# POOL's casts of the tokens of batches 4 to 7, put behind VectorE's last probabilities

## The chip, the cores and the metric

The kernel runs on one core of a Trainium2 chip. The metric is the device time of one execution in microseconds, the median of several runs. The engines of the core have a queue each and work in the order of their queue: TensorE (PE, matmuls; PEld is its weight load), VectorE (DVE), ScalarE (ACT), GpSimd (POOL) and SyncE (SP, which here only issues DMAs). They wait for one another through semaphores. The DMA engines, 16 of them, serve what SP, ACT and POOL issue.

## What is computed

A cross attention between 512 tokens and 32 state rows, for 8 batches of 8 heads with 64 elements each, and behind it a two-layer network over all rows:

```python
scores = scale * x @ state.T          # per batch and head: 512 x 32
a = softmax(scores);   xread = a @ state
scores2 = scale * state @ x.T         # 32 x 512
a2 = softmax(scores2); sread = a2 @ x
rows = concat([xread, sread], axis=2) # 544 rows per batch, heads side by side: 512 wide
h = rows @ w_in                       # 512 -> 2048
out = maximum(0.01 * h, h) @ w_out    # 2048 -> 512
```

Inputs and output are fp32; the kernel multiplies in bf16 and sums in fp32.

## The kernel before

Tokens are laid out with 128 partitions. For each batch the kernel does five things.

1. *Tokens.* `load_x` (L102) brings a batch's fp32 tokens (1 MB) into one of two buffers `xl`; `cast_all` (L135, POOL) casts them to bf16 into one of four buffers `xb`; `a_xt_dma` (L234, issued by SP) transposes those by DMA into one of two buffers `xT`.
2. *Scores.* `a_scores` (L256) multiplies `xT` with the transposed state into PSUM, all heads at once, 32 rows per head.
3. *Two softmaxes of these scores.* Over the state rows: `a_shift` (L266 to L276, VectorE), `a_exp` (L283, ScalarE), `a_probs` (L288 to L298, VectorE), which gives `aT`. Over the tokens: `a_max2` (L316, VectorE), `a_exp2` (L322, ScalarE), `a_probs2` (L330, L332, and L340 once per half, VectorE), which gives `a2`. `a_a2t` (L347, SP) transposes `a2` by DMA for `a_sread` (L365), the second attention's product.
4. *M.* `xread` is never formed: `a_m` (L392) multiplies the state with `w_in` into M, in four column blocks, and `m_evict` (L404 for two separate banks, L406 for a pair) casts each block from PSUM to bf16, on VectorE or ScalarE. So the first layer is `aT` times M.
5. *The network.* `ff1` (L413) makes one of 16 blocks of the hidden layer, with the leaky ReLU on ScalarE (L418); `piece` (L441) adds four of its blocks into a tile of the output; `y_store` (L450, L457) copies a finished tile out of PSUM and stores it through SP.

The order of every engine's queue is that of the program text: nothing is rescheduled. Batches 0 and 1 are written out by hand. Batches 2 to 7 run in a loop over `b` with 16 steps `s`. Step `s` of pass `b` issues `ff1` of batch b, then whatever stands under that step, then one `piece` of batch b - 1 or b. TensorE's queue is thereby dense, and what prepares the next batch, `nxt` = b + 1, is scattered over the steps:

- s = 0: the load of batch b + 2, on SP's queue in passes 2 and 3 and on POOL's in passes 4 and 5; the transposition of `a2` of batch b
- s = 1: scores of batch b + 1, the last block of M of batch b, `a_shift` and `a_max2` of batch b + 1, and in passes 2 to 5 the cast of batch b + 2
- s = 4, 6, 8: `a_sread` of older batches; in pass 2 also the load of the states of batches 4 to 7 (s = 4), and at s = 8 their cast on POOL (`state_cast`, L210) and their transposition by DMA (`state_t`, L215)
- s = 5 to 7: `a_exp`, `a_exp2`, then `a_probs` and `a_probs2` of batch b + 1
- s = 10: three blocks of M of batch b + 1 and their evictions, two of them on VectorE, the first of these being L404
- s = 13: the transposition of the tokens of batch b + 2

An engine isn't held to the step under which its instruction stands, only to its own queue and to the semaphores. POOL has nothing in the loop but the casts of L135, the state cast of pass 2 and the loads of passes 4 and 5, so it comes to each of them as soon as their data or buffer is there.

Of the kernel before, what the change touches and what calls it, by code (L numbers as in the profile page):

```python
# [9 lines left out]
P = 128  # L10
B, H, S, D = 8, 8, 512, 64
# [8 lines left out]
BF16 = mybir.dt.bfloat16  # L20
# [7 lines left out]
def kernel(  # L28
# [9 lines left out]
    nc = tc.nc  # L38

    consts = ctx.enter_context(tc.tile_pool(name="consts", bufs=1))  # L40
# [59 lines left out]
    def load_x(b, eng):  # L100
        xl[b] = xpool.tile([P, H, NT * D], FP32, name="xl", tag="xl", bufs=2)
        eng.dma_start(xl[b][:], x[b].rearrange("h (p t) d -> p h (t d)", t=NT))  # L102
# [11 lines left out]
    def open_xb(b):  # L114
        if b == 2:
            t = xpool.tile([P, 2, NT, NK, D], BF16, name="xb", tag="xb")
            xs[b] = [t[:, u] for u in range(2)]
        else:
            t = xpool.tile([P, NT, H, D], BF16, name="xb", tag="xb")
            xs[b] = [t[:, :, NK * u:NK * (u + 1)] for u in range(2)]  # L120
        xt[b] = t
# [9 lines left out]
            xl[b][:, h0:h1].rearrange("p h (t d) -> p h t d", t=NT),  # L131
        )

    def cast_all(b):
        nc.gpsimd.tensor_copy(  # L135
            xt[b][:].rearrange("p t h d -> p h t d"),
            xl[b][:].rearrange("p h (t d) -> p h t d", t=NT),
        )
# [61 lines left out]
    def load_state(i):  # L200
        lo, hi = groups[i]
        for k in range(NK):
            for g in range(2):
                nc.sync.dma_start(
                    stf[i][NS * k:NS * (k + 1), :, D * g:D * (g + 1)],
                    state[lo:hi, 2 * k + g].rearrange("b n d -> n b d"),
                )
# [6 lines left out]
    def state_t(i):  # L214
        nc.sync.dma_start_transpose(st_t[i][:], stb[i][:].rearrange("p b q -> p (b q)"))  # L215
# [36 lines left out]
    def a_scores(a):  # L252
        sc = psum.tile([P, 2, S], FP32, name="sc", tag="sc", bufs=1)
        for k in range(NK):
            for g in range(2):
                nc.tensor.matmul(  # L256
                    sc[NS * k:NS * (k + 1), g, :],
                    lhsT=st_of(a, g, k),
                    rhs=a.xTh[k // 2][D * g:D * (g + 1), :, k % 2, :],
                    start=True, stop=True,  # L260
                )
        a.sc = sc
# [40 lines left out]
    def a_shift(a):  # L303
        flat = a.sc[:].rearrange("p g c -> p (g c)")
        a.sh = block_sub(flat, block_max(flat, NB), NB)
# [8 lines left out]
    def a_max2(a):  # L314
        a.m2 = att.tile([P, 2], FP32, name="mcol", tag="mcol")
        nc.vector.tensor_reduce(out=a.m2[:], in_=a.sc[:], axis=AX.X, op=ALU.max, negate=True)  # L316
# [12 lines left out]
    def a_probs2(a):  # L329
        nc.vector.tensor_scalar(out=a.r2[:], in0=a.r2[:], scalar1=1e-9, scalar2=None, op0=ALU.add)  # L330
        q2 = att.tile([P, 2], FP32, name="qc", tag="qc")
        nc.vector.reciprocal(q2[:], a.r2[:])  # L332
        if a.b in (0, 6):
            pairs[a.b] = att.tile([P, 2, 2, S], BF16, name="a2p", tag="a2p", bufs=1)
        if a.b in (0, 1, 6, 7):
            a.a2 = pairs[a.b - a.b % 2][:, a.b % 2]
        else:
            a.a2 = att.tile([P, 2, S], BF16, name="a2", tag="a2", bufs=1)[:]
        for g in range(2):
            nc.vector.tensor_scalar(  # L340
                out=a.a2[:, g, :], in0=a.e2[:, g, :],
                scalar1=q2[:, g:g + 1], scalar2=None, op0=ALU.mult,
            )

    def a_a2t(a):
        t = att.tile([P, 2, NT, P], BF16, name="a2T", tag="a2T", bufs=1)
        nc.sync.dma_start_transpose(  # L347
            t[:].rearrange("p g i q -> p (g i) q"), a.a2.rearrange("p g s -> p (g s)")
        )
        a.a2T = t[:]  # L350

    def a_a2t_pair(b):
        t = att.tile([P, 2, 2, NT, P], BF16, name="a2pT", tag="a2pT", bufs=1)
        nc.sync.dma_start_transpose(
            t[:].rearrange("p b g i q -> p (b g i) q"),
            pairs[b][:].rearrange("p b g s -> p (b g s)"),
        )
        for v in range(2):
            att_of[b + v].a2T = t[:, v]
# [20 lines left out]
    def a_m(a, c, tag):  # L380
        if c == 0:
            a.M = mpool.tile([P, 2, DFF], BF16, name="M", tag="M")
        if tag in ("ph", "py", "phpy"):
            pm = [psum.tile([P, DM], FP32, name="pm", tag=t) for t in (tag[:2], tag[-2:])]
            at = [t[:] for t in pm]
        else:
            pm = psum.tile([P, 2, DM], FP32, name="pm", tag=tag, bufs=1)
            at = [pm[:, g, :] for g in range(2)]
        for k in range(NK):
            for g in range(2):  # L390
                v, r = (k // 2, 2 * (k % 2) + (g ^ (k // 2))) if a.b == 0 else (g, k)
                nc.tensor.matmul(  # L392
                    at[v][NS * r:NS * (r + 1)],
                    lhsT=st_of(a, g, k),
                    rhs=w_in_bf[D * g:D * (g + 1), k, DM * c:DM * (c + 1)],
                    start=True, stop=True,
                )
        return pm

    def m_evict(a, c, pm, copy):  # L400
        cols = slice(DM * c, DM * (c + 1))
        if isinstance(pm, list):
            for g in range(2):
                copy(a.M[:, g, cols], pm[g][:])  # L404
        else:
            copy(a.M[:, :, cols], pm[:])  # L406
# [3 lines left out]
    def ff1(a, hT, j):  # L410
        ph = psum.tile([P, S], FP32, name="ph", tag="ph")
        for g in range(2):
            nc.tensor.matmul(  # L413
                ph[:], lhsT=a.M[:, g, P * j:P * (j + 1)],
                rhs=a.aT[:, g, :],
                start=(g == 0), stop=(g == 1),
            )
        nc.scalar.activation(out=hT[:, j, :], in_=ph[:], func=AF.Prelu, scale=1 / SCALE, alpha=0.01)  # L418
# [387 lines left out]
    for b in range(2, B):  # L806
        hT = hpool.tile([P, 16, S], BF16, name="hT", tag="hT")
        a = att_of[b]
        nxt = att_of[b + 1] if b + 1 < B else None
        order = [(b - 1, i, 3) for i in range(2)]  # L810
        order += [(b - 1, i, jq) for i in range(2, NT) for jq in range(4)]
        order += [(b, i, jq) for jq in range(3) for i in range(2)]
        for s in range(16):
            ff1(a, hT, s)
            if s == 0:
                if b + 2 < B:
                    load_x(b + 2, nc.sync if b < 4 else nc.gpsimd)
                    open_xb(b + 2)
                if b == 7:
                    a_a2t_pair(6)  # L820
                elif b != 6:
                    a_a2t(a)
            elif s == 1:
                if nxt is not None:
                    a_scores(nxt)
                m_evict(a, 3, a_m(a, 3, "big"), SCA)
                if nxt is not None:
                    a_shift(nxt)
                    a_max2(nxt)
                if b + 2 < B:  # L830
                    cast_all(b + 2)
            elif s == 4:
                if b == 2:
                    load_state(1)
                    a_sread(a0)
            elif s == 6:
                if b in (2, 7):
                    a_sread(a1 if b == 2 else att_of[6])
            elif s == 8:
                if b != 6:  # L840
                    a_sread(a)
                if b == 2:
                    state_cast(1, nc.gpsimd)
                    state_t(1)
            if nxt is not None:
                if s == 5:
                    a_exp(nxt)
                elif s in (6, 7):
                    a_exp2(nxt, s - 6)
                    if s == 7:  # L850
                        a_probs(nxt)
                        a_probs2(nxt)
                elif s == 10:
                    pm0 = a_m(nxt, 0, "big")
                    pm2 = a_m(nxt, 2, "phpy")
                    pm1 = a_m(nxt, 1, "sc")
                    m_evict(nxt, 2, pm2, VEC)
                    m_evict(nxt, 0, pm0, VEC)
                    m_evict(nxt, 1, pm1, SCA)
                if s == 13 and b + 2 < B:  # L860
                    a_open(att_of[b + 2], b + 2)
                    a_xt_dma(att_of[b + 2])
            pb, i, jq = order[s]
            piece(pb, hT if pb == b else h_prev, i, jq)
        h_prev = hT
# [4 lines left out]
    b = B - 1  # L870
# [43 lines left out]
```

## Time and profile before

| | |
|---|---|
| runs before, us | 214.63, 214.82, 219.38 |
| median, us | 214.82 |
| profiled execution, us | 216.14 |
| its span, us | 214.1 |
| granted TensorE clock | 1.0 |
| HBM read, written | 17.30 MB, 8.91 MB |
| DMA, mean over the span | 129 GB/s |

The span runs from the first to the last instruction in the profile of one execution; the 2 us beside it lie before and behind them. Busy time of an engine, from the first part of the page: TensorE 206.1 us, VectorE 99.7, ScalarE 139.2, POOL 25.6. In a row of the timeline stand the start in us from the span's start, the duration in us, the engine, the line, the operation, the tile written <- the tiles read, the shapes and the number of instructions merged in the row; in square brackets, the engine's idle time before it and what ended that. In a row of grouped instructions stand the least, the median and the greatest duration in ns, then the first and the last start. SPq is SyncE's queue of DMA issues: its duration is that of the issue, not of the transfer. A row "DMA to landing" counts from the start of the issue to the landing.

### The profile page before, as it was taken

How to read it: one execution, taken by the hardware profiler on the slowest of the kernel's cores; microseconds unless marked ns; L12 is line 12 of the kernel's file. 1: busy time of each engine (PE TensorE's matmuls, PEld its weight loads, DVE VectorE, ACT ScalarE, POOL GpSimd, SP SyncE). 2: the span in 40 equal slices, each digit the busy share in tenths (PEclk: the TensorE clock that was granted, in tenths of full speed). 3: DMA queues.
4: the chain of work that ended last, by engine and by line, in shares of the span. 5: the costliest groups of instructions: out<-in, count | busy, mean ns of one | idle time of the engine just before them, and what ended most of it. 6: DMA issues, size and time to landing. Idle time of an engine off the chain costs nothing.

```text
span 214.1 us, 3696 instructions
## 1 busy us (share of the span) xinstructions
PE 206.1 (96%) x1485; PEld 96.4 (45%) x1510; DVE 99.7 (47%) x149; ACT 139.2 (65%) x263; POOL 25.6 (12%) x39
## 2 busy tenths in 40 slices
PE   7889999999999999989999999999999999999994
PEld 2533434343454444434454444444444444466643
DVE  2656797696959146951775085706581000000001
ACT  3578685898787477846696478747774766454420
POOL 8814000030032004503000000000000000000000
PEclk9999999999999999999999999999999999999999
DMA  6999999984962896387215221322023110111123
GB/s 192 211 207 298 254 253 126 239 226 100 240 157 75 176 258 189 139 237 157 95 52 133 64 100 52 91 56 99 35 74 90 52 73 25 49 52 49 49 52 98
DMA packets 38400, 27.70 MB, mean 129 GB/s; under 512 B 24560, under 2 KB 33136, under 8 KB 38384
## 3 DMA queue, kind: packets, MB, share of 16 engines
q1 hardware_dynamic: 32624, 18.75, 36.0%
q0 software_dynamic: 5376, 8.39, 17.7%
q10 hardware_dynamic: 384, 0.33, 0.7%
q8 instruction: 12, 0.20, 0.4%
q14 instruction: 4, 0.03, 0.1%
HBM read 17.30 MB, written 8.91 MB: 122 GB/s over the span
## 4 chain that ended last, share of the span: by engine, by line
PE 88%; DVE 4%; DMA 2%; ACT 2%; issue 1%; SPq 1%; ACTq 0%; DVEq 0%
PE py L441 48%; PE ph L413 21%; PE ph L424 3%; PE pyw L441 3%; PE pm L392 3%; DMA xf<-in_x_dram 2%; PE ph L661 2%; PE pyh L466 2%; PE psr L365 2%; PE php L661 1%; PE sc L256 1%; DVE r L330 1%; SPq L65 1%; PE scn L530 1%; DVE qb L297 1%
## 5 line engine op out<-in xcount | busy, mean ns | idle before, releaser
L441 PE MATMUL py<-w_out_bf,hT 128*128 128x512 bf16 x446 | 116.5, 379 | 1.6 <-DVE M L404 0.5
L418 ACT ACTIVATE hT<-ph 128x512 bf16<-128x512 f32 x112 | 66.5, 602 | 42.4 <-PE ph L413 41.7
L441 PEld LDWEIGHTS <-hT 128*128 128x128 bf16 x496 | 46.7, 98 | 57.6 <-issue 6.1
L413 PE MATMUL ph<-aT,M 128*128 128x512 bf16 x221 | 64.9, 379 | 0.2
L413 PEld LDWEIGHTS <-M 128*128 128x128 bf16 x224 | 21.7, 98 | 27.0 <-issue 1.4
L450 ACT COPY ysb<-py 128x512 f32<-128x512 f32 x31 | 18.1, 585 | 10.7 <-PE py L441 10.7
L266 DVE TRANSPOSE_TENSOR_REDUCE mrow<-sc 128x32 f32<-128x1024 f32 x7 | 8.8, 1250 | 33.2 <-PE sc L256 33.2
L471 DVE COPY ysh<-pyh 128x384 f32<-128x384 f32 x1 | 0.6, 558 | 49.0 <-PE pyh L466 49.0
L135 POOL CAST xb<-xl 128x2048 bf16<-128x2048 f32 x5 | 9.7, 1941 | 61.9 <-DMA xl<-in_x_dram 61.9
L288 DVE TRANSPOSE_TENSOR_REDUCE r<-e 128x32 f32<-128x1024 bf16 x7 | 8.7, 1245 | 11.5 <-ACT e L283 11.5
L406 ACT CAST M<-pm 128x1024 bf16<-128x1024 f32 x13 | 13.2, 1013 | 1.2 <-PE pm L392 0.7
L322 ACT ACTIVATE e<-sc,mcol 128x512 bf16<-128x512 f32 x16 | 11.2, 706 | 0.0
L316 DVE TENSOR_REDUCE mcol<-sc 128x2 f32<-128x1024 f32 x8 | 9.7, 1214 | 0.0
L428 ACT ACTIVATE hs<-ph 128x256 bf16<-128x256 f32 x16 | 6.0, 384 | 4.6 <-PE ph L424 4.4
L297 DVE STREAM_TRANSPOSE qb<-qh 128x1024 bf16<-128x1024 bf16 x7 | 8.7, 1246 | 0.2
L274 DVE STREAM_TRANSPOSE mrowb<-mrow 128x1024 f32<-128x1024 f32 x7 | 8.7, 1245 | 0.2
L276 DVE TENSOR_TENSOR sh<-sc,mrowb 128x1024 f32<-128x1024 f32 x7 | 8.6, 1224 | 0.2
L406 DVE CAST M<-pm 128x1024 bf16<-128x1024 f32 x7 | 8.5, 1216 | 0.2 <-PE pm L392 0.2
L424 PE MATMUL ph<-sr_t,w_in_bf 128*128 128x256 bf16 x64 | 8.3, 273 | 0.0
L404 DVE CAST M<-pm 128x512 bf16<-128x512 f32 x10 | 6.4, 684 | 3.2 <-PE pm L392 3.2
L392 PE MATMUL pm<-w_in_bf,st_t 64*32 64x512 bf16 x192 | 7.6, 379 | 0.0
L441 PE MATMUL pyw<-w_out_bf,hT 128*128 128x512 bf16 x31 | 7.5, 379 | 0.1
(103 smaller groups left out, 159.1 us busy)
## 6 DMA issues: line engine op xcount, KB each, us to landing
out_dram<-ysb SPq DMA_DIRECT2D x31, 256.0 KB, 2.4
xl<-in_x_dram SPq DMA_DIRECT2D x3, 1024.0 KB, 6.8
w_in_bf<-in_moe_w_in_dram POOLq DMA_DIRECT2D x4, 512.0 KB, 9.6
xl<-in_x_dram POOLq DMA_DIRECT2D x2, 1024.0 KB, 6.8
xf<-in_x_dram SPq DMA_DIRECT2D x4, 256.0 KB, 4.1
w_out_bf<-in_moe_w_out_dram POOLq DMA_DIRECT2D x4, 256.0 KB, 13.4
x<-in_x_dram POOLq DMA_DIRECT2D x2, 512.0 KB, 14.4
w_out_bf<-in_moe_w_out_dram POOLq DMA_DIRECT2D x2, 512.0 KB, 15.4
```

The source lines that it names most:

```text
L135: nc.gpsimd.tensor_copy(xt[b][:].rearrange("p t h d -> p h t d"), xl[b][:].rearrange("p h (t d) -> p h t d", t=NT),)
L266: nc.vector.tensor_reduce(out=m1[:], in_=flat.rearrange("p (c j) -> p c j", j=NS), axis=AX.X, op=ALU.max, apply_transpose=True,)
L297: nc.vector.transpose(q1b[:], q1h[:, :, None].to_broadcast([P, n, NS]))
L316: nc.vector.tensor_reduce(out=a.m2[:], in_=a.sc[:], axis=AX.X, op=ALU.max, negate=True)
L322: nc.scalar.activation(out=a.e2[:, g], in_=a.sc[:, g, :], func=AF.Exp, bias=a.m2[:, g:g + 1], accum_out=a.r2[:, g:g + 1],)
L392: nc.tensor.matmul(at[v][NS * r:NS * (r + 1)], lhsT=st_of(a, g, k), rhs=w_in_bf[D * g:D * (g + 1), k, DM * c:DM * (c + 1)], start=True, st ...
L406: copy(a.M[:, :, cols], pm[:])
L413: nc.tensor.matmul(ph[:], lhsT=a.M[:, g, P * j:P * (j + 1)], rhs=a.aT[:, g, :], start=(g == 0), stop=(g == 1),)
L418: nc.scalar.activation(out=hT[:, j, :], in_=ph[:], func=AF.Prelu, scale=1 / SCALE, alpha=0.01)
L424: nc.tensor.matmul(ph[:, :n], lhsT=w_in_bf[:, k, P * j:P * (j + 1)], rhs=sr_t[:, k, :], start=(k == 0), stop=(k == NK - 1),)
L441: nc.tensor.matmul(y.py, lhsT=hT[:, j, P * i:P * (i + 1)], rhs=w_out_bf[:, j, :], start=(j == 0), stop=(j == 15),)
L450: copy(ysb[:], ys[b, i].py)
```

## The change

`cast_all` gets a second argument. Where it is given, POOL first copies it into a one-column tile `turn` that nobody reads, and then casts. The call in the loop moves from step 1 to step 7, behind `a_probs2(nxt)`, and hands over the last column of `a2` of batch b + 1, so POOL's copy waits until VectorE has written it, and the cast comes behind the copy in POOL's queue. Batch 3's cast, ahead of the loop, is as it was.

```diff
+    turn = consts.tile([P, 1], BF16, name="turn")
+
-    def cast_all(b):
+    def cast_all(b, behind=None):
+        if behind is not None:
+            nc.gpsimd.tensor_copy(turn[:], behind)
         nc.gpsimd.tensor_copy(
             xt[b][:].rearrange("p t h d -> p h t d"),
             xl[b][:].rearrange("p h (t d) -> p h t d", t=NT),
...
             elif s == 1:
...
                 if nxt is not None:
                     a_shift(nxt)
                     a_max2(nxt)
-                if b + 2 < B:
-                    cast_all(b + 2)
...
                     if s == 7:
                         a_probs(nxt)
                         a_probs2(nxt)
+                        if b + 2 < B:
+                            cast_all(b + 2, nxt.a2[:, 1, S - 1:])
```

On POOL's queue the four casts keep their places among the state cast and the two loads: batch 4's cast, the state cast, batch 5's cast, the load of batch 6, its cast, the load of batch 7, its cast. On SP's queue nothing moves.

## The prediction

> **What bounds the kernel now.** I read the chain of waits first.
>
> ```profile
> PE 88%; DVE 4%; DMA 2%; ACT 2%; issue 1%; SPq 1%; ACTq 0%; DVEq 0%
> ```
>
> TensorE sets the end, so a change pays only where TensorE stands still, and costs only where it makes it stand. The list of waits, narrowed to TensorE, has one entry in the loop over batches:
>
> ```profile
> PE py L441 <- DVE M L404: 0.5, 1, 0.5
> ```
>
> It happens once. Which batch? The timeline of TensorE, scores of batches 4, 5 and 6 (start, duration):
>
> ```profile
> 77.08 0.41 PE L256 MATMUL sc<-xT,st_t 64*32 64x512 bf16 x8
> ...
> 100.50 0.41 PE L256 MATMUL sc<-xT,st_t 64*32 64x512 bf16 x8
> ...
> 123.23 0.41 PE L256 MATMUL sc<-xT,st_t 64*32 64x512 bf16 x8
> ```
>
> The loop's pass b = 3 takes 100.50 - 77.08 = 23.42 us, pass b = 4 takes 22.73 us with the same matmuls. The difference, 0.69 us, is what can be won in pass 3. Its cause stands in VectorE's timeline: pass 2 (its first line), pass 3, pass 4.
>
> ```profile
> 61.41 1.25 DVE L288 TRANSPOSE_TENSOR_REDUCE r<-e 128x32 f32<-128x1024 bf16 x1 [2.59 <-ACT e L283]
> ...
> 84.60 1.25 DVE L288 TRANSPOSE_TENSOR_REDUCE r<-e 128x32 f32<-128x1024 bf16 x1 [2.12 <-ACT e L283]
> ...
> 88.38 1.86 DVE L330 TENSOR_SCALAR r<-r 128x2 f32<-128x2 f32 x1
> ...
> 91.31 1.27 DVE L404 CAST M<-pm 128x512 bf16<-128x512 f32 x2
> ...
> 108.02 1.25 DVE L288 TRANSPOSE_TENSOR_REDUCE r<-e 128x32 f32<-128x1024 bf16 x1 [2.12 <-ACT e L283]
> ...
> 112.19 0.62 DVE L340 TENSOR_SCALAR a<-e,qc 128x512 bf16<-128x512 bf16 x2
> 113.97 1.29 DVE L404 CAST M<-pm 128x512 bf16<-128x512 f32 x2 [1.17 <-PE pm L392]
> ```
>
> And POOL's:
>
> ```profile
> 62.02 1.89 POOL L135 CAST xb<-xl 128x2048 bf16<-128x2048 f32 x1 [17.06 <-DMA xl<-in_x_dram]
> 66.92 1.50 POOL L210 TENSOR_SCALAR stb<-stf 128x512 bf16<-128x512 f32 x1 [3.01 <-DMA stf<-in_state_dram]
> 79.93 1.89 POOL L135 CAST xb<-xl 128x2048 bf16<-128x2048 f32 x1 [11.51 <-DMA xl<-in_x_dram]
> 81.77 0.97 POOL L102 DMA_DIRECT2D xl<-in_x_dram  x1
> 88.06 2.15 POOL L135 CAST xb<-xl 128x2048 bf16<-128x2048 f32 x1 [5.32 <-DMA xl<-in_x_dram]
> 90.15 0.89 POOL L102 DMA_DIRECT2D xl<-in_x_dram  x1
> 97.75 1.89 POOL L135 CAST xb<-xl 128x2048 bf16<-128x2048 f32 x1 [6.71 <-DMA xl<-in_x_dram]
> ```
>
> The cast that starts at 88.06 is batch 6's, two passes ahead of its use: POOL's queue has nothing in front of it but a landing. It ends at 90.21, and the two-element instruction of L330 that began at 88.38 ends at 90.24. The groups say how odd that is:
>
> ```profile
> L330 DVE TENSOR_SCALAR r<-r x8: 159/160/1858, 37.7 to 157.2; 128x2 f32<-128x2 f32 x8
> ```
>
> ```profile
> L340 DVE TENSOR_SCALAR a<-e,qc x8: 335/354/751, 49.4 to 112.5; 128x512 bf16<-128x512 bf16 x8
> ```
>
> ```profile
> L404 DVE CAST M<-pm x10: 675/681/692, 67.8 to 159.6; 128x512 bf16<-128x512 f32 x10
> ```
>
> L330 takes 0.16 us in the median and 1.86 us once. A VectorE instruction of this kind stands until POOL's cast is through. M's first eviction (L404) in pass 3 would have started 113.97 - 100.50 = 13.47 us after the scores, at 90.55; it started at 91.31, 0.76 us late. TensorE had about 0.07 us of slack there, and 0.69 us reached it.
>
> **The change, part by part.** *The cast leaves VectorE's path.* VectorE's probabilities, undisturbed, run from L288 to the end of L340 in 112.81 - 108.02 = 4.79 us. In pass 3 they end at 84.60 + 4.79 = 89.39, before M's eviction can start (90.55): the 0.69 us goes. Next in line there is TensorE itself, as in pass 4, whose 22.73 us have no such wait. The gain happens once; passes 4 and 5 had no cast beside VectorE's probabilities, and for pass 2, where the cast of 62.02 fell among them too, the list of TensorE's waits has no entry.
>
> *What it adds.* A one-column POOL copy and its wait, four times. The nearest row is a small copy at the start:
>
> ```profile
> 2.25 0.21 POOL L89 COPY zeroed<-ident 128x32 bf16<-128x32 bf16 x1
> ```
>
> 0.21 us, or nothing at the other end; I take 0.21. The release from VectorE has no row; from POOL to SyncE it is 0.03 us (66.92 + 1.50 = 68.42 against 68.45 below). The cast then takes its 1.89 us. In pass 3 it ends at 89.39 + 0.03 + 0.21 + 1.89 = 91.52, against 81.82 before (79.93 + 1.89): 14.44 us behind the scores, in passes 3, 4 and 5 alike. It lies beside M's evictions; this costs nothing, because the state cast on POOL (66.92 to 68.42) lay over the first L404 (67.8), and no L404 left 675 to 692 ns.
>
> *What is queued behind.* On POOL: pass 2's state cast, and the loads of batches 6 and 7. Each load is issued as soon as the cast ahead of it is done, and no longer a pass early. On SyncE the transposition of the freshly cast tokens (L234) now waits for the cast:
>
> ```profile
> 68.45 1.72 SPq L215 DMA_TRANSPOSE st_t<-stb  x1
> 70.26 0.53 SPq L457 DMA_DIRECT2D out_dram<-ysb  x1
> 70.89 2.08 SPq L234 DMA_TRANSPOSE xT<-xb  x1
> ...
> 90.62 6.01 SPq L234 DMA_TRANSPOSE xT<-xb  x1
> ```
>
> ```profile
> L234 SPq DMA_TRANSPOSE xT<-xb x5: 1691/2081/6011, 45.0 to 136.8; - x5
> ...
> DMA to landing us min/median/max: 4.3/4.4/8.7
> ```
>
> Pass 2: probabilities end at 61.41 + 4.79 = 66.20, the cast at 68.33, the state cast at 69.83 at the latest (its 1.50 us lay over a 751 ns L340, so it may be shorter). The state's transposition goes from 68.45 to 69.86, the tokens' from 70.89 to 72.30, and lands 4.4 us later at 76.70. The scores want it at 77.08: 0.38 us of slack at this upper bound, so nothing.
>
> Pass 3 and pass 4 are the tight ones. The transposition of batch 5 (then 6) and the load of batch 6 (then 7) now start together, at 91.52. Before, one such meeting is on record: a load issued at 90.15, a transposition at 90.62 that needed 8.7 us instead of 4.4 and landed at 99.32, 1.57 us after the load (97.75). The transposition gets little done until the load is through. The load took 88.06 - 81.77 = 6.29 us undisturbed and 97.75 - 90.15 = 7.60 us in that meeting. So the transposition lands, after the cast's end: 4.4 us if it were not held at all, 6.29 + 1.57 = 7.86 us with the quick load, 7.60 + 1.57 = 9.17 us with the slow one. The scores of the next batch want it at 77.08 + 22.73 = 99.81, which is 8.29 us after the cast's end. I take the quick load: the output store that went out with the slow one precedes this one by over a microsecond. It lands at 99.38, 0.43 us in time, and TensorE doesn't wait. At the slow end it is 0.88 us late, in each of the two passes. In pass 5 there is no load beside it: issued at 137.67, landed at 142.07, wanted at 123.23 + 22.73 = 145.96.
>
> The Trainium skill, "DMA: Bandwidth & Descriptors", section "Anatomy of one DMA — SWDGE (gpsimd) path", fits such a POOL-issued load by 2.0 us and its bytes over 436 GB/s: for the 128 x 2,048 fp32 of the cast's row (1 MB) an estimate of 4.4 us. By it the transposition would land near 97.5, and the whole 0.69 us would be safe with 2.3 us to spare; the trace disagrees, with 6.29 and 7.60 us.
>
> The sum: -0.69 us, nothing added. The profiled execution took 216.14 us for a span of 214.1; it would become 215.45 and 213.4. That execution lies 1.32 us above the median of the three runs (214.82), so against the median: 214.1, or 214.2 with a little allowed for a transposition that is just late.
>
> **The rivals.** *Late tokens (no gain, or slower).* The meeting of load and transposition is the slow one in both passes. For it: the only recorded meeting was slow, and now the two start even closer together. Against: the load in that meeting shared the queues with an output store. Full price: -0.69 + 2 x 0.88 = +1.07, or 215.9; it decides from 8.29 us after the cast's end on, and with 0.35 us late each time it just eats the gain.
>
> *M's evictions blocked (slower).* The cast now lies from 89.63 to 91.52 over L404, wanted at 90.55. If POOL held VectorE there as it held L330, L404 would be 0.97 us late, of which TensorE takes 0.90, in passes 3, 4 and 5; in pass 2 the cast ends at 68.33 against 67.83, 0.43 us. Together 3 x 0.90 + 0.43 - 0.69 = +2.44: 217.3. It decides from 0.07 us of delay on. Against it are the unmoved L404 beside the state cast, and their narrow group. The Trainium skill, "SBUF — State Buffer", section "Who interferes with whom", counts copies and casts of VectorE among what can contend with GpSimd for a shared port pair, and L404 is a cast; it also makes this depend on conditions, which the trace suggests L404, reading PSUM, doesn't meet.
>
> *Nothing changes.* The cast of batch 6 wasn't the cause, or the 0.69 us comes back as another wait later: 214.8. Against it is the end of L330 within 0.03 us of the cast's.
>
> **How the numbers follow.** Forecast, gain kept: 0.55, with 213.9 to 214.6. Late tokens: 0.27, up to 215.9. Evictions blocked: 0.08, 217.3. Nothing: 0.10, 214.8. The time is 214.2; the range 213.8 to 215.9 leaves out the blocked evictions and the tails. A measurement of this kernel tells about 2%, 4.3 us, from no change, and no case reaches that: faster by more 0.01, within 0.97, slower by more 0.02 (blocked evictions together with a disturbed set of runs, like the 219.38 among those before).
>
> **What would show it.** L330 at 0.16 us in all eight; POOL's cast 14.4 us behind the scores of batches 4, 5, 6; scores of batch 4 to batch 5 in 22.73 us. L404 still under 0.70 us says the evictions aren't blocked. The transpositions of batches 5 and 6 decide the rest: landings up to 8.3 us after the cast, and the scores' L256 then starts on time, straight behind TensorE's work before it. Wrong would be a pass over 23 us between scores, above all passes 3 and 4, or L215's transposition so late in pass 2 that batch 4's scores move.

## The result: 20 us slower, and the profile after

| | before | after |
|---|---|---|
| median, us (6 runs each) | 215.5 | 235.72 |
| lowest, highest, us | 214.63, 219.72 | 233.24, 240.27 |
| ratio, 95% interval | | 1.0921 [1.0861, 1.0981] |
| profiled execution, us | 216.14 | 236.13 |
| its span, us | 214.1 | 234.4 |

The ratio leaves out the runs in a slower state, 219.38 and 219.72 us before and 240.27 us after, so it isn't the quotient of the two medians.

The chain of waits of the changed kernel has a large new member, DMA, with 14% where it had 2%:

```profile
PE 76%; DMA 14%; DVE 5%; POOL 2%; ACT 1%; issue 1%; POOLq 0%; DVEq 0%; ACTq 0%
```

The list of waits, narrowed to TensorE, names it, the transposition of the tokens, and where it stands (engine, line, releaser: us in total, times, longest us):

```profile
PE sc L260 <- DMA xT<-xb: 16.7, 2, 9.1
```

L260 is `a_scores`, L256 before. The timeline of TensorE in the changed kernel shows which scores, those of batches 4, 5, 6 and 7:

```profile
76.45 0.41 PE L260 MATMUL sc<-xT,st_t 64*32 64x512 bf16 x8
...
106.82 0.63 PE L260 MATMUL sc<-xT,st_t 64*32 64x512 bf16 x8 [7.58 <-DMA xT<-xb]
...
140.80 0.63 PE L260 MATMUL sc<-xT,st_t 64*32 64x512 bf16 x8 [9.11 <-DMA xT<-xb]
...
165.67 0.41 PE L260 MATMUL sc<-xT,st_t 64*32 64x512 bf16 x8
```

Passes 3, 4 and 5 take 30.37, 33.98 and 24.87 us, together 21.03 more than three times the 22.73 us of an undisturbed pass. Of these, 7.58 + 9.11 = 16.69 us are the two waits. The rest follows them: TensorE's clock drops. In these rows of the stretches of the changed kernel (from:to, length, busy us of PE, PEld, DVE, ACT and POOL, then the granted clock, the DMA share and GB/s), the first lies ahead of the first wait and the other three behind it:

```profile
96.00:99.00 3.00, 3.00 (x16) 1.27 (x13) 0.00 (x0) 1.30 (x3) 0.00 (x0) 1.00 1.09 124
106.80:110.00 3.20, 3.18 (x22) 0.95 (x23) 2.45 (x2) 1.24 (x2) 0.00 (x0) 0.50 0.27 95
110.00:113.00 3.00, 3.00 (x13) 1.23 (x12) 2.40 (x3) 1.55 (x3) 0.00 (x0) 0.81 0.22 87
113.00:116.00 3.00, 3.00 (x16) 1.35 (x15) 0.00 (x0) 1.75 (x3) 0.00 (x0) 1.00 0.00 0
```

A clock of 0.50 over 3.20 us and of 0.81 over 3.00 us loses 1.60 + 0.57 = 2.17 us. TensorE falls back by as much: 24.87 - 22.73 = 2.14 us in pass 5, which has no wait of its own, and 33.98 - 22.73 - 9.11 = 2.14 us in pass 4 beside its wait. So about 16.7 us are waiting and 4.3 us the slow clock behind it.

The queues show what met. First POOL's timeline in the changed kernel:

```profile
88.94 0.19 POOL L138 COPY turn<-a 128x1 bf16<-128x1 bf16 x1 [19.82 <-DVE a L344]
89.07 1.89 POOL L139 CAST xb<-xl 128x2048 bf16<-128x2048 f32 x1
90.90 0.97 POOL L102 DMA_DIRECT2D xl<-in_x_dram  x1
121.40 0.18 POOL L138 COPY turn<-a 128x1 bf16<-128x1 bf16 x1 [29.52 <-DVE a L344]
121.52 1.89 POOL L139 CAST xb<-xl 128x2048 bf16<-128x2048 f32 x1
123.36 0.89 POOL L102 DMA_DIRECT2D xl<-in_x_dram  x1
```

And SyncE's, the transpositions of batches 5 and 6 alone:

```profile
90.99 2.38 SPq L238 DMA_TRANSPOSE xT<-xb  x1
...
123.44 3.33 SPq L238 DMA_TRANSPOSE xT<-xb  x1
```

Each load starts 0.08 to 0.09 us ahead of the transposition. The first transposition takes 15.8 us to land, where 4.4 was the median before (its tile's row for pass 3):

```profile
DMA to landing us min/median/max: 15.8/15.8/15.8
```

The load beside it takes 15.8 us too, and in pass 4 the two take 17.3 and 17.2. VectorE's part came out as forecast: no instruction of L334 (L330 before) is stretched, and none of M's evictions (L408, L404 before).

```profile
L334 DVE TENSOR_SCALAR r<-r x8: 157/160/161, 37.0 to 177.0; 128x2 f32<-128x2 f32 x8
```

```profile
L408 DVE CAST M<-pm x10: 680/686/693, 67.2 to 179.3; 128x512 bf16<-128x512 f32 x10
```

### The profile page after: what moved, and what is told of

The parts are those of the page before. It is cut to its first block, busy times and chain, and to the rows that moved or that the text cites. A ratio compares the mean times of both kernels' runs of the same rounds, so it can differ in the third digit from the quotient of the medians.

```text
span 234.4 us, 3728 instructions
## 1 busy us (share of the span) xinstructions
PE 212.3 (91%) x1510; PEld 97.7 (42%) x1510; DVE 96.3 (41%) x149; ACT 139.5 (60%) x263; POOL 26.0 (11%) x43
## 4 chain that ended last, share of the span: by engine, by line
PE 76%; DMA 14%; DVE 5%; POOL 2%; ACT 1%; issue 1%; POOLq 0%; DVEq 0%; ACTq 0%
PE py L445 39%; PE ph L417 17%; DMA xT<-xb 14%; PE pyw L445 3%; PE ph L428 3%; PE pm L396 3%; PE ph L665 2%; POOL xb L139 2%; PE pyh L470 1%; PE sc L260 1%; PE pspin L168 1%; PE php L665 1%; PE psr L369 1%; DVE qb L301 1%; DVE r L292 1%; DVE aT L302 1%
## 5 line engine op out<-in xcount | busy, mean ns | idle before, releaser
L445 PE MATMUL py<-w_out_bf,hT 128*128 128x512 bf16 x464 | 121.3, 386 | 0.0
L445 PEld LDWEIGHTS <-hT 128*128 128x128 bf16 x496 | 47.4, 99 | 59.6 <-issue 9.5
L417 PE MATMUL ph<-aT,M 128*128 128x512 bf16 x224 | 66.4, 384 | 0.0
L260 PE MATMUL sc<-xT,st_t 64*32 64x512 bf16 x48 | 2.9, 459 | 16.7 <-DMA xT<-xb 16.7
L292 DVE TRANSPOSE_TENSOR_REDUCE r<-e 128x32 f32<-128x1024 bf16 x7 | 8.7, 1246 | 15.3 <-ACT e L287 15.3
L408 DVE CAST M<-pm 128x512 bf16<-128x512 f32 x10 | 6.4, 686 | 5.7 <-PE pm L396 5.7
L260 PEld LDWEIGHTS <-st_t 64*32 64x32 bf16 x48 | 0.7, 91 | 19.4 <-DMA xT<-xb 17.7
L138 POOL COPY turn<-a 128x1 bf16<-128x1 bf16 x3 | 0.6, 187 | 69.9 <-DVE a L344 69.9
```

Of the source, the lines that this page charges most:

```text
L292: nc.vector.tensor_reduce(out=r1[:], in_=e1[:].rearrange("p (c j) -> p c j", j=NS), axis=AX.X, op=ALU.add, apply_transpose=True,)
L417: nc.tensor.matmul(ph[:], lhsT=a.M[:, g, P * j:P * (j + 1)], rhs=a.aT[:, g, :], start=(g == 0), stop=(g == 1),)
L445: nc.tensor.matmul(y.py, lhsT=hT[:, j, P * i:P * (i + 1)], rhs=w_out_bf[:, j, :], start=(j == 0), stop=(j == 15),)
```

## The experiments

Theory: the load on POOL's queue and the transposition on SyncE's, starting together, slow each other (they crawl, for short), and this is all that costs. Rivals: the casts' new place itself; VectorE starving POOL's loads; any overlap of load and transposition; any second queue. A kernel whose result has no ratio was run once; the kernel before, run beside it, had medians of 214.75 to 215.99 us. The diffs show the lines that matter. Where one sends `load_x(b + 3, ...)` for `b in (3, 4)`, step 0 no longer issues these two loads.

### Taking the meeting away

Loads on SyncE's queue, where they are issued behind the transposition (`sp_loads`):

```diff
-                    load_x(b + 2, nc.sync if b < 4 else nc.gpsimd)
+                    load_x(b + 2, nc.sync)
```

> The changed kernel, but with the loads of batches 6 and 7 on SyncE's queue, where they stand behind the transposition of the tokens and cannot meet it. Theory (load and transposition crawl when they meet on two queues): the transpositions of batches 5 and 6 land 4.4 us after their issue, the scores don't wait, all of the 20 us goes and the 0.69 us of VectorE's stretched probabilities is kept: 214.1 us, passes 3 and 4 in 22.7 us between scores. Rival (the casts' new place itself costs, by a later transposition or by what POOL does beside VectorE): still 225 us or more.

Measured: 215.43 us against 214.75, ratio 1.0024 [1.0009, 1.0038]. Transpositions land after 4.2 to 4.4 us, no wait of the scores is left, and the passes take 22.72 to 22.73 us:

```profile
76.55 0.41 PE L260 MATMUL sc<-xT,st_t 64*32 64x512 bf16 x8
...
99.27 0.41 PE L260 MATMUL sc<-xT,st_t 64*32 64x512 bf16 x8
...
122.00 0.41 PE L260 MATMUL sc<-xT,st_t 64*32 64x512 bf16 x8
```

The whole 20 us hung on the loads' queue, with the casts in their new place. But the time isn't the 214.1 us expected: with both passes clean, it still isn't below the kernel before. Why it stays 0.24% above wasn't found: nearly all its executions have spans of 213.0 to 213.6 us where 8 of 13 of the kernel before have 212.6 or 212.7, and no wait in the loop says why. The profiled execution shows where, at least: against `before_again`, below, its scores of batch 4 come 0.26 us later (76.55 against 76.29), and 2.6 us lie behind the issue of its last store, against 2.2.

Loads on POOL's queue, but behind the transposition (`load_behind_xt`):

```diff
+                    if b >= 4:
+                        nc.gpsimd.tensor_copy(turn[:], att_of[b + 1].xT[:, 0, 0, :1])
                     load_x(b + 2, nc.sync if b < 4 else nc.gpsimd)
```

> The changed kernel, with a one-column POOL copy ahead of the loads of batches 6 and 7 that waits until the transposition of the tokens just cast has landed. The loads stay on POOL's queue, some 4.5 us later. Theory (the meeting): transposition 4.4 us, load 6.3 us, 214.1 us as with the loads on SyncE. Rival (loads from POOL's queue are slow wherever they stand from now on, because VectorE starves the writing of their descriptors): loads still above 12 us, but no wait of the scores.

Measured: 214.4 us in one run. The transpositions take 4.3 us, the loads 6.0 and 6.1. POOL's queue isn't slow by itself; VectorE is idle for the first 3.6 us of the first load here, though, so the rival with VectorE is answered by the next pair.

### Moving the transposition against the load

The load is issued first; then the cast is done n times more (`cast_again` is the cast alone), which keeps the transposition waiting (n = 1: `xt_1_later`, n = 3: `xt_3_later`).

```diff
                             cast_all(b + 2, nxt.a2[:, 1, S - 1:])
+                            if b in (3, 4):
+                                load_x(b + 3, nc.gpsimd)
+                                open_xb(b + 3)
+                                for _ in range(n):
+                                    cast_again(b + 2)
```

> The changed kernel, with batch 5's and 6's cast done a second time behind the issue of the load, so that the transposition is issued some 2.8 us behind the start of the load's issue, and not beside it. Theory (who is first decides: a load that is under way keeps its pace and the transposition waits behind it, as in the one meeting of the kernel before): load 6.3 to 7.6 us, transposition landed about 1.6 us behind the load, waits of the scores under 1.5 us in each pass, 214 to 217 us. Rival (any overlap of the two crawls): both above 12 us again, 230 us or more.

> As the run before, with three more casts in place of one: the transposition is issued some 6.6 us behind the start of the load's issue, when the load has nearly landed. VectorE does beside the load what it does in the changed kernel. Theory (the meeting): load 6.3 us, transposition 4.4 us, landed about 11 us behind the first cast's end and thereby some 2.7 us late for the scores in each of two passes, 219 to 220 us. Rival (VectorE's evictions beside the load starve its descriptors): load above 12 us as in the changed kernel.

Measured: 214.98 us and 225.67 us, one run each. With one more cast the load lands in 6.3 and 6.2 us and the transposition, issued 2.91 and 2.82 us behind it, in 5.2 and 5.1; no pass waits. So overlap alone isn't it. With three, 5.8 and 4.3 us in pass 3, and the waits are the 2.7 us expected:

```profile
PE sc L266 <- DMA xT<-xb: 5.6, 2, 2.8
```

The load has beside it what VectorE does in the changed kernel, and takes 5.7 to 5.8 us, so VectorE doesn't starve it. The time is 6 us above what I expected, though. Part of it is this execution's start, which came to the scores of batch 4 2.44 us later than `xt_1_later` (78.79 against 76.35); its granted clock was 0.50 from 8.5 to 11.8 us. Another part is what follows a wait: pass 5, without a wait of its own, takes 24.32 us, 1.59 more than 22.73, after a wait of only 2.74 us, and pass 4 has 1.49 us beside its wait.

What the engines do in the meeting, in the changed kernel first and in `xt_1_later` second (same columns as above):

```profile
95.00:105.00 10.00, 4.24 (x20) 1.75 (x18) 0.00 (x0) 2.88 (x5) 0.00 (x0) 0.97 1.16 115
```

```profile
92.50:98.50 6.00, 5.95 (x28) 2.74 (x28) 0.00 (x0) 2.94 (x5) 1.19 (x1) 1.00 1.02 267
```

The packets fill the DMA engines' time in both (1.16 and 1.02; the share adds up what the packets took, so it can pass 1), but move 115 against 267 GB/s. The packets themselves took longer: the 256-byte packets of the transpositions 60 ns in the mean in pass 3 of the changed kernel, and 22 ns in `load_behind_xt`.

### Without a moved cast

The kernel before, with its loads of batches 6 and 7 alone held, a pass earlier in the text than step 0 had them: behind M's first eviction (`loads_alone`),

```diff
                     m_evict(nxt, 2, pm2, VEC)
+                    if b in (3, 4):
+                        nc.gpsimd.tensor_copy(turn[:], nxt.M[:, 1, 3 * DM - 1:3 * DM])
+                        load_x(b + 3, nc.gpsimd)
```

or behind `turn` and three small POOL copies (`unmoved_same`; six in `unmoved_later`):

```diff
                         a_probs2(nxt)
+                        if b in (3, 4):
+                            nc.gpsimd.tensor_copy(turn[:], nxt.a2[:, 1, S - 1:])
+                            for _ in range(3):
+                                nc.gpsimd.tensor_copy(junk[:], xl[b + 2][:, 0])
+                            load_x(b + 3, nc.gpsimd)
```

> The kernel before with its casts where they were; only the loads of batches 6 and 7 are moved, behind a one-column POOL copy that waits for the first eviction of M in passes 3 and 4, so that they start about 1.5 us behind the transposition of the tokens of batches 5 and 6. Theory (a transposition that is first and a load that comes from another queue crawl together): load and transposition above 12 us, waits of the scores of some 7 to 9 us in each of two passes, 230 to 237 us with the casts unmoved. Rival (the moved casts are part of the cause): 215 us.

> The kernel before with its casts where they were; only the loads of batches 6 and 7 are held, behind VectorE's last probabilities and some 1 us of small POOL copies that nobody reads, so that they start within about 0.5 us of the transposition. The run loads_alone started them 1.4 to 1.9 us behind it, when it was through before their first packets came, and nothing crawled. Theory (a crawl needs load packets that arrive while a transposition is half done): load and transposition above 12 us in passes 3 and 4, 228 us or more, with no cast moved. Rival (the moved casts are part of the cause): transposition under 9 us, 216 us or less.

> As the run before with twice the small copies, the loads some 1 us later, about 1 us behind the transposition. Theory: its first packets come 2 to 3 us after its issue, when the transposition has had 2 to 3 us of data: either the crawl, shorter than with the start together, or none; between 215 and 230 us. Rival as for the run before: 216 us or less in both.

Measured: 215.17, 224.88 and 215.79 us. `loads_alone` missed the meeting: its loads came 1.4 and 1.9 us behind the transposition and neither crawled, against my expectation. `unmoved_later`'s came 1.88 and 1.23 us behind, and neither crawled. `unmoved_same` hit the meeting, in one pass of two. Its POOL and SyncE rows, pass 4 last in each:

```profile
91.23 0.97 POOL L102 DMA_DIRECT2D xl<-in_x_dram  x1 [0.20 <-issue]
...
114.00 0.89 POOL L102 DMA_DIRECT2D xl<-in_x_dram  x1
```

```profile
90.75 2.00 SPq L237 DMA_TRANSPOSE xT<-xb  x1
...
114.15 3.15 SPq L237 DMA_TRANSPOSE xT<-xb  x1
```

In pass 3, where the load is 0.48 us behind, the two take 9.1 and 9.4 us and the scores wait 0.16. In pass 4, where it is 0.15 us ahead, they take 15.3 and 15.8 and the scores wait 7.06. No cast was moved: the moved casts are only what brought the two starts together.

### Another queue, and how narrow the moment is

Loads from ScalarE's queue: behind its eviction of M (`act_loads`, without the copy below), at s = 11 (`act_later`, likewise), and behind a one-column copy that waits for the cast (`act_same`):

```diff
                     m_evict(nxt, 1, pm1, SCA)
+                    if b in (3, 4):
+                        nc.scalar.copy(mark[:], xt[b + 2][:, NT - 1, H - 1, D - 1:])
+                        load_x(b + 3, nc.scalar)
```

> The changed kernel, with the loads of batches 6 and 7 issued from ScalarE's queue behind its eviction of M in passes 3 and 4, near the moment at which POOL issues them in the changed kernel. Theory (any load on another queue than the transposition's): the same crawl, both above 12 us, 228 us or more. Rival (only loads whose descriptors POOL writes): load 7 us or less, transposition under 6 us, 214 to 216 us.

> The changed kernel, with the loads of batches 6 and 7 on ScalarE's queue one step later than in act_loads, where the load was 0.7 us ahead and kept its pace (6.3 us, transposition 7.4 us). Now it starts about 1 us behind the transposition. Theory (order decides, on whatever queue): load and transposition above 12 us, 228 us or more. Rival (the crawl needs POOL's software queue): load under 8 us, transposition under 8 us, 214.5 to 217 us.

> The changed kernel, with the loads of batches 6 and 7 on ScalarE's queue, behind a one-column ScalarE copy that waits for the cast, so that load and transposition are set off by the same event, as in the changed kernel, and start within 0.3 us of each other. The two earlier runs with ScalarE's queue were 0.7 us ahead and 0.6 us behind. Theory (the crawl belongs to the load on POOL's queue): load under 8 us, transposition under 9 us, 215 to 218 us. Rival (starting together is enough, on any two queues): both above 12 us, 228 us or more.

Measured: 215.33, 218.85 and 215.8 us, with no wait of the scores in any. `act_later` reached the scores of batch 4 some 3 us late already (79.83, against 76.32 in `act_loads`); its passes take 22.72 to 22.73 us. In `act_same` the load starts 0.07 and 0.09 us behind the transposition and takes 6.0 us, the transposition 7.6:

```profile
91.23 4.40 SPq L239 DMA_TRANSPOSE xT<-xb  x1
91.29 0.20 ACT L867 COPY mark<-xb 128x1 bf16<-128x1 bf16 x1
91.30 0.40 ACTq L102 DMA_DIRECT2D xl<-in_x_dram  x1
```

In the four passes of the two other runs the load was 0.71 to 0.77 us ahead and 0.58 to 0.59 us behind; it took 6.3 to 7.0 us and the transposition 7.3 to 7.6. So issues that start nearly together aren't enough on any two queues, and what I had expected of `act_loads` and `act_later`, a crawl with the load on any queue, didn't come: the crawl was seen with POOL's loads alone. ScalarE's a tenth of a microsecond ahead wasn't tried. The start of the issue isn't that of the data, however: POOL's issue takes 0.9 to 1.0 us here and ScalarE's 0.4. The first packets, behind the table below, settle more.

One or two more one-column copies ahead of POOL's load (`pool_1_copy`, `pool_2_copies`):

```diff
+                    if b >= 4:
+                        for _ in range(n):
+                            nc.gpsimd.tensor_copy(turn[:], xl[b + 1][:, 0, :1])
                     load_x(b + 2, nc.sync if b < 4 else nc.gpsimd)
```

> The changed kernel with one more one-column POOL copy between the cast and the load, so that the load starts 0.1 to 0.3 us later against the transposition than in the changed kernel (where it is 0.09 us ahead). Theory (a narrow window around starting together): still the crawl if the window reaches past 0.2 us behind, with landings of 12 us or more and 225 us or more; else as unmoved_same in pass 3, 0.5 us behind, 9 us each and 215 to 217 us. Rival (a start together is not the condition, and the 0.5 us case was chance): any mix.

> As the run before, with two copies, 0.3 to 0.5 us later. Theory: out of the window, as 0.48 us behind was: landings 8 to 10 us, waits under 1.5 us, 215 to 218 us. Rival: crawl, 228 us or more.

Measured: 222.12 and 214.96 us, the first being the mix that the rival named. One copy moves the load to 0.04 us behind the transposition and leaves 8.8 and 8.4 us in pass 3, 12.4 and 12.4 in pass 4; two copies move it to 0.77 and 0.41 us behind, with transpositions of 6.9 and 8.2 us and no wait. Two copies of one column, some 0.4 us of POOL's time, take away 20 us.

One meeting instead of two (`one_meeting`):

```diff
-                    load_x(b + 2, nc.sync if b < 4 else nc.gpsimd)
+                    load_x(b + 2, nc.gpsimd if b == 4 else nc.sync)
```

> The changed kernel with the load of batch 7 on SyncE's queue, that of batch 6 still on POOL's. Theory (each meeting costs by itself): the transposition of batch 5 lands after 15 to 17 us and that of batch 6 after 4.4, about half of the loss is left, 222 to 227 us. Rival (the second meeting was a result of the first): 214.7 or 235 us.

Measured: 225.26 us, one wait of 7.64 us. Each meeting costs by itself.

The meetings of a POOL load with the transposition of the tokens within 3 us, in the order of the start of the load's issue against that of the transposition's. The last column is the start of the load's first packet in the trace against that of the transposition's first; where it is negative, the load's data came first.

| load against transposition, us | kernel, pass | load, us | transposition, us | first packets, us |
|---|---|---|---|---|
| -2.91 | xt_1_later, 3 | 6.3 | 5.2 | -3.22 |
| -2.82 | xt_1_later, 4 | 6.2 | 5.1 | -3.13 |
| -1.92 | before_again, 3 | 8.4 | 9.0 | -4.48 |
| -0.47 | before, 3 | 7.6 | 8.7 | -1.74 |
| -0.15 | unmoved_same, 4 | 15.3 | 15.8 | 0.65 |
| -0.09 | after, 3 | 15.8 | 15.8 | 1.64 |
| -0.09 | one_meeting, 3 | 15.9 | 15.8 | 1.76 |
| -0.08 | after, 4 | 17.2 | 17.3 | 2.04 |
| 0.04 | pool_1_copy, 3 | 8.8 | 8.4 | 2.92 |
| 0.04 | pool_1_copy, 4 | 12.4 | 12.4 | 2.40 |
| 0.41 | pool_2_copies, 4 | 8.6 | 8.2 | 2.88 |
| 0.48 | unmoved_same, 3 | 9.1 | 9.4 | 2.89 |
| 0.77 | pool_2_copies, 3 | 8.2 | 6.9 | 2.73 |
| 1.23 | unmoved_later, 4 | 8.6 | 8.1 | 2.62 |
| 1.39 | loads_alone, 4 | 8.0 | 8.1 | 2.59 |
| 1.88 | unmoved_later, 3 | 7.1 | 4.4 | 2.70 |
| 1.91 | loads_alone, 3 | 7.0 | 4.5 | 2.71 |

The first packets sort the rows better than the issues do. Where the load's come 0.65 to 2.40 us behind the transposition's, all five meetings crawl, with 12.4 us or more; from 2.59 us on, and where the load's come first, none takes more than 9.4. They answer for ScalarE too: in `act_same` its load's packets were 2.2 us ahead, so this wasn't the same meeting, but in `act_later` they were 1.48 and 1.50 us behind, inside that stretch, and nothing crawled. ScalarE's load has 1,024 packets of 1 KB, though, and POOL's 256 of 4 KB: whether the queue or the size of its packets makes the crawl isn't shown.

### The kernel before once more, and the best version

A second profile of the kernel before (`before_again`):

> The kernel before, unchanged, for a second profile. The 13 runs of it beside the last kernels had spans of 212.6 to 213.4 us, the profiled one 214.1, and the kernels without a wait in passes 3 and 4 have 212.6 to 213.3 as well. Theory (the cast of batch 6 fell among VectorE's probabilities only in the profiled execution, by the moment at which its load landed, so that most executions had no 0.69 us to win): L330 at 0.16 us in all eight and all passes at 22.7 us. Rival (the collision is in every execution): L330 once above 1 us and pass 3 at 23.4 us.

Measured: 214.67 us, span 212.6. Pass 3 takes 22.72 us. The cast of batch 6 fell among VectorE's probabilities here too, but 1.2 us earlier against them (2.27 us behind the start of L288, and 3.46 in the first profile), and M's eviction wasn't late, 13.47 us behind the scores (76.29) as in an undisturbed pass:

```profile
86.08 1.89 POOL L135 CAST xb<-xl 128x2048 bf16<-128x2048 f32 x1 [5.18 <-DMA xl<-in_x_dram]
86.97 1.53 DVE L298 TENSOR_TENSOR aT<-e,qb 128x1024 bf16<-128x1024 bf16 x1
...
89.76 1.29 DVE L404 CAST M<-pm 128x512 bf16<-128x512 f32 x2
```

L298 takes 1.53 us instead of 0.69, and L330 at most 0.34 us. So neither answer is right as I put it: the collision is there, but its price varies with the moment, and in this execution it is nothing.

The casts held as in the change, and the loads sent ahead of them, behind VectorE's row maxima (`loads_early`):

```diff
                     a_max2(nxt)
+                if b in (3, 4):
+                    nc.gpsimd.tensor_copy(turn[:], nxt.m2[:, :1])
+                    load_x(b + 3, nc.gpsimd)
```

> The changed kernel with the loads of batches 6 and 7 taken ahead of the held casts: behind a one-column POOL copy that waits for VectorE's row maxima in passes 3 and 4, some 9 us before the transposition. Theory (the meeting is all that costs): loads 6.3 us, landed before the casts of batches 5 and 6 end, transpositions 4.4 us, all passes 22.7 us, within 0.3 per cent of the kernel before, 214.2 to 214.9 us. Rival (holding the casts costs by itself): above 216 us.

Measured: 214.69 us against 214.97, ratio 0.9984 [0.9972, 0.9995]. The load of batch 6 takes 6.2 us, the transpositions 4.2 to 4.4, the passes of 22.72 to 22.73. It is the one version whose interval lies below the kernel before, by 0.16% in the mean and 0.05% at its end: a small gain.

## Why the prediction was wrong, point by point

*TensorE sets the end, and passes 3 and 4 are the tight ones.* Right: both waits stand there, at the scores of batches 5 and 6, and they are the rival named "late tokens".

*"I take the quick load", with the slow end at 9.17 us and 0.88 us late.* This is the step that failed. It priced the meeting by the one on record, 0.47 us apart, and took that price for the upper bound, although the changed kernel starts the two 0.09 us apart. The prediction named this ("the two start even closer together") and then bounded it from the wrong side: between 0.47 and 0.09 us the price goes from 8.7 to 15.8 us. Its sum was the load, 6.29 or 7.60 us, and 1.57 us more until the transposition lands. The second term came out at next to nothing, as the two landed within 0.3 us of one another. The first was far too small: the load took 15.8 and 17.2 us. The reading behind it, that a transposition gets little done until the load is through, came from a meeting in which the load's first packet was 1.74 us ahead. In the changed kernel the transposition's were ahead, by 1.64 and 2.04 us, and both crawled. In place of 0 to 0.88 us, the waits were 7.58 and 9.11 us.

*What a wait costs.* The prediction counted a late transposition one for one. Behind each wait TensorE ran at half clock at first, which added 2.14 us.

*The 0.69 us to be won.* It was in the profiled execution, and the second profile has none of it. The prediction saw that this execution lay 1.32 us above the median and still took the 0.69 us off the median. Even with the meeting away, `loads_early` gains 0.16%, not 0.3%, and `sp_loads` is 0.24% slower.

*The cast leaves VectorE's path; M's evictions aren't blocked; the copy costs 0.2 us; pass 2 stays in time.* Right: L334 and L408 as quoted, `turn` takes 0.18 to 0.19 us, the cast ends at 90.96, 14.51 us behind the scores (14.44 forecast), and the scores of batch 4 didn't wait.

## What to carry to other kernels

When a change lets one event set off two transfers on different queues, their order and distance are part of the change: look for the nearest meeting in the trace, by the first packets and not only by the issues, and treat a price that was seen at another distance as a point and not as a bound. A gain that is seen in one execution belongs to the time only as far as other executions have it too; compare the profiled span with the spans of the other runs before taking it off their median. And a wait of TensorE of some microseconds costs more than its length: 1.3 to 2.8 us more behind waits of 2.7 to 9.1 us here.

## What the runs showed of the hardware

- A 1 MB load from POOL's queue whose first packets come 0.65 to 2.40 us behind those of a DMA transposition from SyncE's: both take 12.4 to 17.3 us, in all five such meetings, instead of 6.2 and 4.3, and the packets fill the DMA engines' time (a share of 1.16) at 115 GB/s. From ScalarE's queue the same load, 1.48 us behind by the first packets, takes 6.8 us. What happens in the DMA engines stays open. The transposition of `a2`, issued 2 to 3.5 us behind that of the tokens, runs beside every crawl (14.0 us to landing in pass 3 of the changed kernel), and no run leaves it out.
- The starts of the issues alone don't fix the price: 8.8 and 12.4 us for the load at the same 0.04 us.
- The granted clock fell to 0.50 during the wait of 7.58 us and stood there for 4.3 us behind it. A wait of 2.84 us was enough too: in `xt_3_later`, the stretch behind it,

```profile
104.40:107.40 3.00, 2.97 (x21) 0.89 (x22) 2.23 (x2) 1.03 (x2) 0.00 (x0) 0.50 0.46 129
```

  has the same 0.50. What follows a wait doesn't grow with the wait: 1.33 us behind 7.64 (`one_meeting`), 2.77 us behind 4.16 (`pool_1_copy`). The Trainium skill, "TensorE: Matmul & The Clock Gate", section "Part 1: The HAM clock gate (the "warmup" mystery)", has the clock halve after an idle window of about 3.4 us and come back after about as long a busy one; here a wait of 2.84 us, shorter than that, was enough, and TensorE worked at half clock for 3 us behind it, and for 4.3 us in the changed kernel.
